# Float64 weights split in 480 columns instead of 576, with ScalarE and DMA copies taking part; gates multiplied by ScalarE

## The chip, the core and the metric

One core of a Trainium2 chip. The metric is the device time of one execution in microseconds; lower is better. TensorE (PE) multiplies matrices into PSUM, VectorE (DVE), ScalarE (ACT) and GpSimd (POOL) do elementwise work, SyncE (SP) issues DMAs. Every engine has a queue of its own and runs it in order; an instruction that waits holds up all that stand behind it.

## The reference

Three models run one after the other on 3072 tokens of 320 values: a recurrent attention, a mixture of eight experts with 1024 hidden units, and a gated feed-forward model with 1536 hidden units.

```python
def _moe_ref(x, modality_id, w_gate, modality_bias, w1, w2):
    logits = x @ w_gate + modality_bias[modality_id]
    e_idx = np.argmax(logits, axis=1)
    ...
    gate_w = probs[np.arange(N), e_idx]
    for e in range(E):
        mask = e_idx == e
        h = np.maximum(x[mask] @ w1[e], 0.0)
        out[mask] = gate_w[mask, None] * (h @ w2[e])
    return out

def _moe2_ref(x, w_gate, w_val, w_out):
    g = x @ w_gate
    silu = g * (1.0 / (1.0 + np.exp(-g)))
    val = x @ w_val
    return silu * val @ w_out
```

The weights of the last model (`w_gate`, `w_val`: 320 x 1536; `w_out`: 1536 x 320) come in as float64, because numpy's division by a square root makes them so.

## The kernel before

**Order.** The attention takes the first 560 us. Then the experts run in 32 passes `p` (eight slots of tokens, `sj`, by four quarters of the hidden units, `c`), until about 783 us, and then the gated model, in blocks of two or three tiles of 128 tokens and in passes `k` of 128 hidden units each. The program lists the instructions in an order written out by hand, and each engine takes its own from that list.

**Numbers in two parts.** Float32 values are multiplied on TensorE as a high part in a shorter format and the rest: three products of high and low each (`mm3`, lines 607 to 610). The 320 inputs are two blocks of 128 and one of 64; the last 64 fill only half of the partitions. There the high and the low part of `x` stand one above the other (`x2`), and the weights of these 64 inputs stand twice, once in each half of the partitions (`up`, lines 618 and 619). So the weights' third block has the same values in partitions 0 to 63 and 64 to 127.

**Splitting float64 weights.** `moe2_weights` (line 578) cuts each of `w_gate` (g) and `w_val` (v) into eight chunks of 192 hidden units, and `w_out` (o) into six. For each of these 22 chunks SyncE loads the raw words into a tile `st2` of which there are two (lines 591 to 596; the last 64 inputs are loaded twice, line 593), and `split64` (line 557) makes `hi` and `lo` in eight steps `o0` to `o7`. A float64 is two 32-bit words, `hw` and `lw`. ScalarE squares `hw` for a test against tiny values (line 566) and copies the result into the high part (line 572). VectorE builds the float32 from `hw` (567, 568, 571), makes a float of the top bits of `lw` by shifting and setting an exponent (569), takes the exponent (573), scales the low word by it (574), subtracts the high part (575) and adds both to the low part (576). The work tiles `cva`, `cvm`, `cvu` exist once. The load of chunk k+1 stands before step `o2` of chunk k. The steps are dealt out among the passes: in the experts' part by `prepare` (line 952), eleven chunks in all, and in the second model about four steps a pass, one between the cast `hh` (line 1120) and the difference `hl` (line 1124), the others behind it.

**Expert weights.** In each pass SyncE loads the weights of a later one (`load1`, `load2`), ScalarE casts them (line 668), and GpSimd or VectorE makes the difference (line 669). `evac` (line 928) takes the hidden units out of PSUM: ScalarE's Relu (930), VectorE's difference (931). PSUM has two tiles `pu` for hidden units, which the second model uses in turn for `pg` and `pv`: Silu (1115), product (1117), cast (1120), difference (1124).

**Gates.** A block's rows `xg` are gathered by GpSimd (line 973), the row's gate too (979), `gmul` (line 980) multiplies them on VectorE, and `xt2` has TensorE transpose the result (line 652). In the first block of the second model `gmul` and `xt2` for the next block stand in the passes 0 to 3.

Of the kernel before, what the change touches and what calls it, by code (L numbers as in the profile page):

```python
# [7 lines left out]
F32 = mybir.dt.float32  # L8
F32R = mybir.dt.float32r
BF16 = mybir.dt.bfloat16  # L10
I32 = mybir.dt.int32
AF = mybir.ActivationFunctionType
ALU = mybir.AluOpType
AX = mybir.AxisListType
# [487 lines left out]
def routing_constants(tc, keep, rc, mid, mbias):  # L502
# [3 lines left out]
    def tr(shape,name,dt=F32): C[name]=rc.tile(shape,dt,name="r"+name); return C[name]  # L506
    it=tr([128,128],"it",I32)
    G.iota(it[:],pattern=[[1,128]],base=0,channel_multiplier=0)
# [8 lines left out]
    h3=tk([128,NT],"h3",BF16); V.tensor_scalar(h3[:],it[:,0:NT],64.0,None,ALU.add)  # L517
    ip=tr([128,1],"ip",I32); G.iota(ip[:],pattern=[[0,1]],base=0,channel_multiplier=1)
    pp=tk([128,1],"pp"); V.tensor_copy(pp[:],ip[:])
# [8 lines left out]
    mi=tr([128,24],"mi",I32)  # L528
    nc.sync.dma_start(mi[:],mid.bitcast(I32).rearrange("(t p two) -> p t two",p=128,two=2)[:,:,0])
    bb=tr([128,2,8],"bb")  # L530
# [15 lines left out]
def choose(tc, C, LG, t0, t1):  # L546
# [7 lines left out]
    V.tensor_tensor(eq,eq,C['rev'][:].unsqueeze(1).to_broadcast([128,n,8]),ALU.mult)  # L554
    V.tensor_reduce(km,eq,AX.X,ALU.max)
    V.tensor_tensor(oh.rearrange("p e t -> p t e"),eq,bc(km),ALU.is_equal)
def split64(nc, P, raw, hi, lo, shape):

    V,A,G=nc.vector,nc.scalar,nc.gpsimd
    def t(n,dt=I32): return P.tile(shape,dt,tag="cv"+n,bufs=1,name="cv"+n)  # L560
    lw,hw=raw[:,:,:,0],raw[:,:,:,1]
    a,m,u=t("a"),t("m"),t("u")
    k=u[:].bitcast(F32)
    af,mf,uf=a[:].bitcast(F32),m[:].bitcast(F32),u[:].bitcast(F32)
    def o0():
        A.activation(k,hw.bitcast(F32),AF.Square)
        V.tensor_scalar(a[:],hw,3,0x3fffffff,ALU.logical_shift_left,ALU.bitwise_and)
    def o1(): V.scalar_tensor_tensor(a[:],hw,-0x40000000,a[:],ALU.bitwise_and,ALU.bitwise_or)
    def o2(): V.tensor_scalar(m[:],lw,9,0x3f800000,ALU.logical_shift_right,ALU.bitwise_or)
    def o3():  # L570
        V.scalar_tensor_tensor(af,k,3.4332275390625e-05**2,af,ALU.is_ge,ALU.mult)
        A.copy(hi,af)
    def o4(): V.tensor_scalar(u[:],a[:],-0x800000,None,ALU.bitwise_and)
    def o5(): V.scalar_tensor_tensor(mf,mf,-1.0,uf,ALU.add,ALU.mult)
    def o6(): (G if Q["G6"] else V).tensor_tensor(af,af,hi.bitcast(F32),ALU.subtract)
    def o7(): V.scalar_tensor_tensor(lo,mf,2.0**-20,af,ALU.mult,ALU.add)
    return [o0,o1,o2,o3,o4,o5,o6,o7]
def moe2_weights(tc, pool, stp, wg, wv, wo):

    nc=tc.nc  # L580
    W={}; T={}
    for nm,src in (("g",wg),("v",wv)):
        T[nm]=src.bitcast(I32).rearrange("k (f two) -> k f two",two=2)
        W[nm]=tuple(pool.tile([128,3,1536],F32R,name="w"+nm+x) for x in "hl")
    W["o"]=tuple(pool.tile([128,12,320],F32R,name="wo"+x) for x in "hl")
    T["o"]=wo.bitcast(I32).rearrange("k (f two) -> k f two",two=2)
    todo=[(nm,c) for c in range(8) for nm in "gvo" if nm!="o" or c<6]
    def step(k):
        nm,c=todo[k]; hi,lo=W[nm]; src=T[nm]
        if nm!="o":  # L590
            s=stp.tile([128,3,192,2],I32,tag="st2",name="st2"); cs=slice(192*c,192*c+192)
            nc.sync.dma_start(s[:,0:2],src[0:256,cs].rearrange("(k p) f two -> p k (f two)",p=128))
            for z in range(2): nc.sync.dma_start(s[64*z:64*z+64,2],src[256:320,cs])
            return lambda: split64(nc,stp,s,hi[:,:,cs],lo[:,:,cs],[128,3,192])
        s=stp.tile([128,2,320,2],I32,tag="st2",name="st2o"); cs=slice(2*c,2*c+2)
        nc.sync.dma_start(s[:],src[256*c:256*c+256].rearrange("(k p) f two -> p k (f two)",p=128))
        return lambda: split64(nc,stp,s,hi[:,cs],lo[:,cs],[128,2,320])
    def ops():
        nxt=step(0); yield
        for k in range(len(todo)):  # L600
            cur=nxt; nxt=None
            l=cur()
            for i,f in enumerate(l):
                if i==2 and k+1<len(todo): nxt=step(k+1)
                yield f
    return W,ops(),8*len(todo)
# [18 lines left out]
class Moe:  # L625
# [266 lines left out]
    def main(s, LG, y1, gd, wg, wv, wo, out):  # L892
        tc=s.tc; nc=s.nc; V,A,G,T=nc.vector,nc.scalar,nc.gpsimd,nc.tensor; C=s.C
        s.gd=gd
        with ExitStack() as ctx:
# [3 lines left out]
            P=ctx.enter_context(tc.tile_pool(name="m1",bufs=1)); s.wp.append(P)  # L899
# [7 lines left out]
            R={}; GX={}  # L907
# [43 lines left out]
            done=0  # L951
# [14 lines left out]
            XG={}; ID={}; GT={}; YP={}; YT=[]  # L966
# [13 lines left out]
            def gmul(b,i):  # L980
                if b>=len(blocks) or i>=len(blocks[b]): return
                h=blocks[b][i]; t=TILES[h]
                V.tensor_scalar(XG[b][i][:,0:320],XG[b][i][:,0:320],(GT[b][:,i:i+1] if h>=0 else R['gate'][:,t:t+1]),None,ALU.mult)
            def xt2(b,i):
                if b>=len(blocks) or i>=len(blocks[b]): return
                if i==0: X['b',b]=s.xspare(b) if 2<=b<HB else s.xalloc(NSTAT+b)
# [37 lines left out]
            for p in range(NP):  # L1024
                sj,c=divmod(p,4)
# [22 lines left out]
                if sj==NSTAT-1 and c<2: gmul(0,c)  # L1048
# [55 lines left out]
            k=0  # L1104
            for b,h in passes:
                n=128*len(blocks[b]); x=cut(X['b',b],n)
                for fc in ((0,1,2,3,4,5),(6,7,8,9,10,11),range(12))[h]:
# [3 lines left out]
                    while done<8*NEED[fc] and done<nbetween:  # L1111
                        f=next(between,None); done+=1
# [8 lines left out]
                    if done<need(2*NP+k):  # L1121
                        f=next(between,None); done+=1
# [87 lines left out]
```

## Time and profile before

| | |
|---|---|
| median of 3 runs | 1206.11 us (1204.70 to 1207.41) |
| the profiled execution | 1203.11 us |
| its span | 1201.4 us |
| busy: PE, DVE, ACT, POOL | 88%, 68%, 47%, 42% |

The span runs from the first to the last instruction recorded; the rest of an execution's time lies around it. In the rows below a name such as `hl<-pu,hh` says which tile an instruction writes and which it reads; `st` is a raw g or v chunk, `st2o` a raw o chunk, `woh` and `wol` the high and low part of `w_out`. A bracket gives the idle time before an instruction and the one that ended it. "issue" stands where no releaser was found. PEq, DVEq and SPq are sequencers.

### The profile page before, as it was taken

The page shows a single profiled execution, that of the slowest core. Times are in us where ns is not written, and L with a number is a line of the kernel's source. Part 1 is how long each engine was busy: PE and PEld are TensorE (multiplying, and loading weights), DVE is VectorE, ACT ScalarE, POOL GpSimd, SP SyncE. Part 2 cuts the span into 40 slices and gives each one's busy share as a digit, 9 for nine tenths or more (in the row PEclk, how much of TensorE's full clock was granted, in tenths as well). Part 3 has the DMA queues.
Part 4 walks back from the last instruction along what each step waited for, and adds up shares of the span by engine and source line. Part 5 has one row for each costly group of instructions (what it writes and reads, how often), then busy time and mean ns, then how long its engine had stood idle before and what let it go on. Part 6 is the DMA issues. An engine that isn't in the chain of part 4 may idle for free. (4 is left out here: it accounts for less than half of the span.)

```text
span 1201.4 us, 27833 instructions
## 1 busy us (share of the span) xinstructions
PE 1060.6 (88%) x10437; PEld 998.4 (83%) x10437; DVE 822.9 (68%) x2020; ACT 558.8 (47%) x1344; POOL 499.0 (42%) x1038
## 2 busy tenths in 40 slices
PE   5358799898988889897899899979999999999998
PEld 4247788887877778786789899979999999999998
DVE  5998888989889887753837987888952343333332
ACT  4346466756666674453435555444432222222332
POOL 7885666767666575512434343422000311201100
PEclk9668989998899999998999999999999999999999
DMA  5555346554644542330556577432100100100000
GB/s 97 85 91 95 71 79 118 102 118 82 136 98 95 104 89 66 77 86 22 172 150 179 176 212 223 135 107 86 60 1 11 40 22 23 34 1 28 17 24 12
DMA packets 278720, 102.88 MB, mean 86 GB/s; under 512 B 235728, under 2 KB 273360, under 8 KB 278576
## 3 DMA queue, kind: packets, MB, share of 16 engines
q1 hardware_dynamic: 271264, 86.05, 32.1%
q0 software_dynamic: 3856, 11.02, 3.1%
q10 hardware_dynamic: 3456, 3.93, 1.0%
q8 instruction: 86, 1.41, 0.5%
q14 instruction: 58, 0.48, 0.1%
HBM read 77.56 MB, written 23.40 MB: 84 GB/s over the span
## 5 line engine op out<-in xcount | busy, mean ns | idle before, releaser
L1117 DVE TENSOR_TENSOR s<-s,pu 128x384 f32<-128x384 f32 (+1 forms) x108 | 55.0, 509 | 157.3 <-PE pu L619 153.7
L266 POOL TENSOR_TENSOR tmp<-Lb,Pm 128x60 f32<-128x60 f32 (+22 forms) x348 | 107.5, 309 | 53.7 <-DMA Lb<-LD 27.7
L266 DVE TENSOR_TENSOR tmp<-Lb,Pm 128x60 f32<-128x60 f32 (+24 forms) x372 | 112.7, 303 | 19.2 <-DMA Lb<-LD 8.1
L1120 ACT CAST hh<-s 128x384 fp32r<-128x384 f32 (+1 forms) x108 | 51.6, 478 | 149.2 <-DVE s L1117 149.2
L1085 POOL DMA_INDIRECT out_dram<-ys,id x20 | 19.7, 987 | 234.2 <-DVE ys L1082 104.7
L269 DVE TENSOR_TENSOR Pm<-Pm,tmp 128x60 f32<-128x60 f32 (+24 forms) x372 | 108.6, 292 | 9.4
L669 POOL TENSOR_TENSOR l<-s,h 128x768 fp32r<-128x768 f32 (+1 forms) x32 | 59.4, 1859 | 133.8 <-ACT h L668 103.7
L269 POOL TENSOR_TENSOR Pm<-Pm,tmp 128x60 f32<-128x60 f32 (+22 forms) x348 | 102.8, 295 | 26.6 <-POOL tmp L266 0.3
L1115 ACT ACTIVATE s<-pu 128x384 f32<-128x384 f32 (+1 forms) x108 | 49.2, 456 | 112.4 <-PE pu L619 112.1
L608 PE MATMUL pd<-woh,hh 128*128 128x320 f32 x288 | 89.0, 309 | 0.1
L609 PE MATMUL pd<-woh,hl 128*128 128x320 f32 x288 | 89.1, 309 | 0.1
L610 PE MATMUL pd<-wol,hh 128*128 128x320 f32 x288 | 88.9, 309 | 0.0
L1124 DVE TENSOR_TENSOR hl<-s,hh 128x384 fp32r<-128x384 f32 (+1 forms) x108 | 55.4, 513 | 47.9 <-ACT hh L1120 47.4
L198 POOL TENSOR_TENSOR ks<-I,rawb 64x320 f32<-64x320 f32 x48 | 49.4, 1028 | 52.0 <-DVE I L194 30.0
L608 PE MATMUL pu<-xh,h 128*128 128x384 f32 (+1 forms) x128 | 48.8, 381 | 16.8 <-DVE hl L931 11.1
L668 ACT CAST h<-s 128x640 fp32r<-128x640 f32 (+1 forms) x64 | 49.6, 780 | 28.4 <-PE pd L609 9.6
L608 PE MATMUL pd<-h,hh 128*128 128x320 f32 x200 | 61.9, 310 | 0.0
L609 PE MATMUL pd<-h,hl 128*128 128x320 f32 x200 | 61.8, 309 | 0.0
L610 PE MATMUL pd<-l,hh 128*128 128x320 f32 x200 | 61.8, 309 | 0.0
L374 PE MATMUL pq<-rbd,VT 128*128 128x128 f32 x384 | 58.1, 300 | 0.0
L223 PE MATMUL sc<-kbt,atb 128*128 128x128 f32 x384 | 54.4, 296 | 3.6 <-ACT atb L209 2.8
L316 PE MATMUL zz<-pbd,MA 128*104 128x128 f32 x384 | 54.7, 290 | 2.5 <-ACT VU L138 1.0
(377 smaller groups left out, 3400.1 us busy)
## 6 DMA issues: line engine op xcount, KB each, us to landing
s<-in_moe_w_dram SPq DMA_DIRECT2D x32, 320.0 KB, 3.6
s<-in_moe_w_dram SPq DMA_DIRECT2D x32, 256.0 KB, 3.3
Lb<-LD SPq DMA_DIRECT2D x24, 256.0 KB, 3.7
y<-zrow SPq DMA_DIRECT2D x9, 483.0 KB, 4.7
s<-in_moe_w_dram SPq DMA_DIRECT2D x64, 64.0 KB, 3.3
raww<-in_w_dram SPq DMA_DIRECT2D x24, 160.0 KB, 3.3
rawa<-in_a_dram SPq DMA_DIRECT2D x24, 160.0 KB, 3.7
rawk<-in_k_dram SPq DMA_DIRECT2D x24, 160.0 KB, 2.8
```

The source lines that it names most:

```text
L223: T.matmul(ps[:,q].rearrange("p s j -> p (s j)"),ATB[0][:,4*c+q].rearrange("p s j -> p (s j)"),X[i,c][:,q],start=True,stop=True)
L266: E.tensor_tensor(tmp[:,0:k_,0:ni],Lb[:,j+1:32,j].unsqueeze(1).to_broadcast([128,k_,ni]), Pm[:,0:k_,j].unsqueeze(2).to_broadcast([128,k_,n ...
L269: E.tensor_tensor(Pm[:,0:k_,j+1:32],Pm[:,0:k_,j+1:32],tmp[:,0:k_,0:ni],ALU.add)
L316: T.matmul(ps[0:104,h],u['MA'][:,8*i+4*g+h,0:104],pbd[:,4*g+h],start=True,stop=True)
L374: T.matmul(pq[:,q],X['VT',c][:,q],RBD[0][:,q,cc].rearrange("p s t -> p (s t)"),start=True,stop=True)
L608: T.matmul(out,lh,rh,start=first,stop=False)
L609: T.matmul(out,ll,rh,start=False,stop=False)
L610: T.matmul(out,lh,rl,start=False,stop=last)
L669: (E or s.nc.gpsimd).tensor_tensor(hl[1][:],t[:],hl[0][:].bitcast(F32),ALU.subtract)
L1117: V.tensor_tensor(sg,sg,pv,ALU.mult)
L1120: A.copy(hh,sg)
L1124: V.tensor_tensor(hl,sg,hh.bitcast(F32),ALU.subtract)
```

## The change

The split of a g or v chunk works on 480 columns instead of 576: two blocks of 192, and the last 64 inputs as 96 columns, the first 96 hidden units in partitions 0 to 63 and the other 96 in partitions 64 to 127, so that nothing is split twice. The high part goes to a tile `sph` of its own (there is one), the low part of the first 384 columns straight into its place, and that of the 96 columns into the raw tile. SyncE then issues nine copies between SBUF tiles: one of the high part's 384 columns and four of its 96 columns (each half of the hidden units into each half of the partitions) after `o3`, and four of the low part's after `o7`. Step `o7` of a g or v chunk is two VectorE instructions, of 384 and of 96 columns. In all chunks, o too, ScalarE makes a float of the whole low word, read as an unsigned integer, in step `o0`, behind the Square; step `o2` is empty and the scale of `o5` is 2 to the power of -32. `gmul` is a ScalarE instruction.

```diff
--- before.py
+++ after.py
@@ -9,6 +9,7 @@
 F32R = mybir.dt.float32r
 BF16 = mybir.dt.bfloat16
 I32 = mybir.dt.int32
+U32 = mybir.dt.uint32
 AF = mybir.ActivationFunctionType
 ALU = mybir.AluOpType
 AX = mybir.AxisListType
@@ -554,26 +555,32 @@
     V.tensor_tensor(eq,eq,C['rev'][:].unsqueeze(1).to_broadcast([128,n,8]),ALU.mult)
     V.tensor_reduce(km,eq,AX.X,ALU.max)
     V.tensor_tensor(oh.rearrange("p e t -> p t e"),eq,bc(km),ALU.is_equal)
-def split64(nc, P, raw, hi, lo, shape):
+def split64(nc, P, raw, hi, lo, shape, done=None):
 
     V,A,G=nc.vector,nc.scalar,nc.gpsimd
     def t(n,dt=I32): return P.tile(shape,dt,tag="cv"+n,bufs=1,name="cv"+n)
-    lw,hw=raw[:,:,:,0],raw[:,:,:,1]
+    lw,hw=raw[...,0],raw[...,1]
     a,m,u=t("a"),t("m"),t("u")
     k=u[:].bitcast(F32)
     af,mf,uf=a[:].bitcast(F32),m[:].bitcast(F32),u[:].bitcast(F32)
     def o0():
-        A.activation(k,hw.bitcast(F32),AF.Square)
+        A.activation(k,hw.bitcast(F32),AF.Square); A.copy(mf,lw.bitcast(U32))
         V.tensor_scalar(a[:],hw,3,0x3fffffff,ALU.logical_shift_left,ALU.bitwise_and)
     def o1(): V.scalar_tensor_tensor(a[:],hw,-0x40000000,a[:],ALU.bitwise_and,ALU.bitwise_or)
-    def o2(): V.tensor_scalar(m[:],lw,9,0x3f800000,ALU.logical_shift_right,ALU.bitwise_or)
+    def o2(): pass
     def o3():
         V.scalar_tensor_tensor(af,k,3.4332275390625e-05**2,af,ALU.is_ge,ALU.mult)
         A.copy(hi,af)
+        if done: done[0]()
     def o4(): V.tensor_scalar(u[:],a[:],-0x800000,None,ALU.bitwise_and)
-    def o5(): V.scalar_tensor_tensor(mf,mf,-1.0,uf,ALU.add,ALU.mult)
+    def o5(): V.scalar_tensor_tensor(mf,mf,2.0**-32,uf,ALU.mult,ALU.mult)
     def o6(): (G if Q["G6"] else V).tensor_tensor(af,af,hi.bitcast(F32),ALU.subtract)
-    def o7(): V.scalar_tensor_tensor(lo,mf,2.0**-20,af,ALU.mult,ALU.add)
+    def o7():
+        for l,f in lo if done else ((lo,None),):
+            x,y=(mf,af) if f is None else (mf[:,f],af[:,f])
+            if f and f.start==0: x,y=(z.rearrange("p (k f) -> p k f",k=2) for z in (x,y))
+            V.scalar_tensor_tensor(l,x,2.0**-20,y,ALU.mult,ALU.add)
+        if done: done[1]()
     return [o0,o1,o2,o3,o4,o5,o6,o7]
 def moe2_weights(tc, pool, stp, wg, wv, wo):
 
@@ -588,10 +595,19 @@
     def step(k):
         nm,c=todo[k]; hi,lo=W[nm]; src=T[nm]
         if nm!="o":
-            s=stp.tile([128,3,192,2],I32,tag="st2",name="st2"); cs=slice(192*c,192*c+192)
-            nc.sync.dma_start(s[:,0:2],src[0:256,cs].rearrange("(k p) f two -> p k (f two)",p=128))
-            for z in range(2): nc.sync.dma_start(s[64*z:64*z+64,2],src[256:320,cs])
-            return lambda: split64(nc,stp,s,hi[:,:,cs],lo[:,:,cs],[128,3,192])
+
+            s=stp.tile([128,480,2],I32,tag="st2",name="st2"); cs=slice(192*c,192*c+192)
+            nc.sync.dma_start(s[:,0:384].rearrange("p (k f) two -> p k (f two)",k=2),src[0:256,cs].rearrange("(k p) f two -> p k (f two)",p=128))
+            for z in range(2): nc.sync.dma_start(s[64*z:64*z+64,384:480],src[256:320,192*c+96*z:192*c+96*z+96])
+            t=stp.tile([128,480],F32R,tag="sph",bufs=1,name="sph"); t2=s[:,384:432].rearrange("p f two -> p (f two)").bitcast(F32R)
+            def both(y,x):
+                for z in range(2):
+                    for q in range(2):
+                        nc.sync.dma_start(y[64*q:64*q+64,2,192*c+96*z:192*c+96*z+96].bitcast(F32),x[64*z:64*z+64].bitcast(F32))
+            def high():
+                nc.sync.dma_start(hi[:,0:2,cs].bitcast(F32),t[:,0:384].bitcast(F32).rearrange("p (k f) -> p k f",k=2))
+                both(hi,t[:,384:480])
+            return lambda: split64(nc,stp,s,t[:],((lo[:,0:2,cs],slice(0,384)),(t2,slice(384,480))),[128,480],(high,lambda: both(lo,t2)))
         s=stp.tile([128,2,320,2],I32,tag="st2",name="st2o"); cs=slice(2*c,2*c+2)
         nc.sync.dma_start(s[:],src[256*c:256*c+256].rearrange("(k p) f two -> p k (f two)",p=128))
         return lambda: split64(nc,stp,s,hi[:,cs],lo[:,cs],[128,2,320])
@@ -980,7 +996,7 @@
             def gmul(b,i):
                 if b>=len(blocks) or i>=len(blocks[b]): return
                 h=blocks[b][i]; t=TILES[h]
-                V.tensor_scalar(XG[b][i][:,0:320],XG[b][i][:,0:320],(GT[b][:,i:i+1] if h>=0 else R['gate'][:,t:t+1]),None,ALU.mult)
+                A.mul(XG[b][i][:,0:320],XG[b][i][:,0:320],(GT[b][:,i:i+1] if h>=0 else R['gate'][:,t:t+1]))
             def xt2(b,i):
                 if b>=len(blocks) or i>=len(blocks[b]): return
                 if i==0: X['b',b]=s.xspare(b) if 2<=b<HB else s.xalloc(NSTAT+b)
```

## Rows read from the trace of the kernel before

**Rows 1.** The page's forty slices of 30 us: busy tenths, and granted clock.

```profile
PE   5358799898988889897899899979999999999998
DVE  5998888989889887753837987888952343333332
PEclk9668989998899999998999999999999999999999
```

**Rows 2.** Stretch sums; columns: PE, PEld, DVE, ACT, POOL busy, PEclk, DMA share, GB/s.

```profile
740.00:750.00 10.00, 7.79 (x40) 7.52 (x40) 9.34 (x16) 3.53 (x7) 1.90 (x1) 0.83 0.84 249
783.00:810.00 27.00, 20.59 (x156) 19.16 (x154) 21.81 (x49) 11.38 (x26) 6.75 (x6) 1.00 0.39 108
890.00:1201.00 311.00, 307.47 (x2033) 306.64 (x2032) 107.66 (x236) 85.92 (x198) 40.85 (x42) 1.00 0.07 21
```

**Rows 3.** What TensorE waited for, 600 to 900 us: total, times, longest us.

```profile
PE pu L608 <- DVE hl L931: 8.2, 6, 2.3
PE xt L652 <- issue: 6.8, 5, 2.0
PE pu L608 <- ACT s L1115: 1.7, 2, 1.5
```

**Rows 4.** TensorE's timeline: start, length us; in brackets the idle before, releaser.

```profile
688.67 0.44 PE L608 MATMUL pu<-xh,h 128*128 128x384 f32 x1 [1.40 <-DVE hl L931]
745.50 0.44 PE L608 MATMUL pu<-xh,h 128*128 128x384 f32 x1 [2.21 <-DVE hl L931]
796.66 0.52 PE L652 MATMUL xt<-ident,xg 128*128 128x128 f32 x3 [1.75 <-issue]
```

**Rows 5.** VectorE by line: count, min/median/max ns, first and last start, forms.

```profile
L568 DVE SCALAR_TENSOR_TENSOR cva<-st,cva x16: 743/758/2347, 633.3 to 877.8; 128x576 int32<-128x576 int32 x16
L568 DVE SCALAR_TENSOR_TENSOR cva<-st2o,cva x6: 818/826/826, 658.4 to 843.0; 128x640 int32<-128x640 int32 x6
L569 DVE TENSOR_SCALAR cvm<-st x16: 445/453/515, 634.0 to 879.0; 128x576 int32<-128x576 int32 x16
L569 DVE TENSOR_SCALAR cvm<-st2o x6: 484/485/486, 662.7 to 844.4; 128x640 int32<-128x640 int32 x6
L983 DVE TENSOR_SCALAR xg<-xg,gt x20: 374/386/389, 765.4 to 1071.7; 128x320 f32<-128x320 f32 x20
```

**Rows 6.** ScalarE by line, the same columns.

```profile
L566 ACT ACTIVATE cvu<-st x16: 717/729/737, 632.0 to 874.6; 128x576 f32<-128x576 f32 x16
L566 ACT ACTIVATE cvu<-st2o x6: 774/782/799, 655.9 to 840.6; 128x640 f32<-128x640 f32 x6
L572 ACT CAST wgh<-cva x8: 672/674/678, 635.2 to 872.2; 128x576 fp32r<-128x576 f32 x8
L942 ACT COPY ys<-pd x16: 425/428/448, 605.0 to 787.7; 128x320 f32<-128x320 f32 x16
L819 ACT ACTIVATE H<-H,rpp x2: 759/760/760, 579.5 to 580.9; 128x552 bf16<-128x552 bf16 x2
```

**Rows 7.** Timelines of VectorE and GpSimd at 742 us.

```profile
741.95 2.28 DVE L576 SCALAR_TENSOR_TENSOR wvl<-cvm,cva 128x576 fp32r<-128x576 f32 x1
...
741.71 1.90 POOL L669 TENSOR_TENSOR l<-s,h 128x768 fp32r<-128x768 f32 x1 [2.31 <-ACT h L668]
```

**Rows 8.** Issue, line 593; then us to landing of lines 943 and 596.

```profile
L593 SPq DMA_DIRECT2D st<-in_moe_w_val_dram x16: 479/595/859, 623.6 to 863.5; - x16
...
DMA to landing us min/median/max: 2.1/2.9/3.6
...
DMA to landing us min/median/max: 4.0/5.1/7.6
```

**Rows 9.** VectorE's timeline: end of one chunk, start of the next but one.

```profile
804.46 0.76 DVE L576 SCALAR_TENSOR_TENSOR wgl<-cvm,cva 128x576 fp32r<-128x576 f32 x1
...
815.14 0.48 DVE L567 TENSOR_SCALAR cva<-st2o 128x640 int32<-128x640 int32 x1
```

**Rows 10.** DMA queue, 630 to 900 us: packets, MB, share of 16 engines.

```profile
q1 hardware_dynamic: 26128, 31.63, 39.1%
```

## Prediction

> **What bounds the kernel now.** I read the page's forty slices first [rows 1]: TensorE falls to seven tenths in slice 27 and is at nine from slice 28 on, and VectorE is at seven to nine tenths in slices 22 to 29, where the change's code runs. The stretch sums [rows 2] show that TensorE works 307.5 of the last 311 us, so nothing done there to the other engines can move the end; but in the first block of the second model, 783 to 810 us, it works 20.6 of 27 us while VectorE works 21.8. So I asked what TensorE waits for between 600 and 900 us [rows 3]: 8.2 us for `hl` of line 931, which frees the PSUM tile, 6.8 us before the transposes `xt`, put down to "issue" but standing behind the gate multiply that makes their input, and 1.7 us for the Silu. That is 16.7 us, all that a lighter VectorE can give. Single waits [rows 4] show where: 1.40, 2.21, 1.75 us. Everything after 823 us moves with the sum of what is saved before.
>
> **What VectorE loses.** Its eight split instructions have two rates [rows 5]: two-tensor ones (lines 568, 571, 574, 575, 576) take 758 ns at 576 columns and 826 at 640, 1.06 ns a column, so 656 at 480, 554 at 384, 248 at 96; the scalar ones (567, 569, 573) take 453 and 485, so 405 at 480. A g or v chunk costs 5 x 758 + 3 x 453 = 5149 ns. Afterwards: 4 x 656, 554 + 248 for line 576 cut in two, 2 x 405, line 569 gone: 4236 ns. That is 0.913 us less on each of 16 chunks, 14.6 us; the six o chunks lose line 569's 485 ns, 2.9 us; eleven of the 24 gate multiplies at 386 ns lie before 890 us, 4.2 us. VectorE gets 21.7 us lighter while it matters. Most of that lies beside TensorE's work and saves nothing; only what stands in front of a wait counts.
>
> **What ScalarE gains.** The Square falls from 729 to 649 ns (0.83 ns a column from its two rows [rows 6]), the cast to `hi` from 674 to 594. The conversion of the low word isn't in the trace; its nearest row is the Square, which reads the same strided words: 649 ns at 480, 782 at 640. If conversion from unsigned integers cost nothing extra it could be as short as the cast, 594; the other bound is twice the Square, 1.3 us. I take 649. Per g or v chunk ScalarE gets 0.49 us more, per o chunk 0.78. The gate multiply lies between the plain copy of 320 columns, 428 ns, and line 819's multiply by a per-partition scale, 760 ns at 552 columns, so 567 at 320; I take 567, the same form. ScalarE works 11.4 of 27 us in the first block [rows 2], so the time is there; its order is what can cost.
>
> **The sum, 632 to 783 us.** I followed VectorE's queue back from each `hl` wait to the last point where it idled, and subtracted the split instructions between: 0.5 us at 675, 0.25 at 681, 0.85 at 689 (a whole g chunk stands there, and the wait is 1.40), 0.53 at 695, 0.24 at 703, 0.2 at 745, 0.4 at 766: 3.0 us. At 766 the transposes would no longer wait 1.6 us for the multiply, but `hl` of line 931 frees the PSUM tile 0.4 us later and is late next.
>
> At 745 VectorE's line 576 took 2.28 us because GpSimd's line 669 began just before it [rows 7]; other VectorE instructions of two SBUF tensors stretch likewise. The Trainium skill (SBUF — State Buffer, Who interferes with whom) says that the two engines lock a shared port pair for a whole instruction and that the first to issue wins; the trace agrees in this pair. By that rule cutting line 576 in two opens a gap in which GpSimd may get in, an estimated 1.9 us when it does; by my sum, without it, the cut costs 0.04 us a chunk.
>
> **The sum, 783 to 823 us.** The wait of 0.81 us at 791 grows by 0.4: the multiply now stands on ScalarE behind the cast to `hi`, itself behind VectorE's line 571 (0.73 + 0.57 against the 0.39 and 0.49 saved). At 797 the multiply no longer stands behind three split instructions on VectorE; the 1.75 us go but for 0.25, where `s` of line 1117 is late next: 1.5. At 802, line 569 and the shorter forms save 0.7 and the move another 0.7: 1.4. The Silu waits at 806 to 810 have 1.28 us of removed work in front of them: 1.2. Together 1.5 + 1.4 + 1.2 - 0.4 = 3.7 us. The wait of 0.67 us at 823 is for the gathered gate itself and stays, now on ScalarE with the next Silu queued behind it.
>
> **What the new order takes back.** Nine more DMAs a chunk go through SyncE: five wait for `hi`, four for the low part; queued behind them are the expert weights, the y stores and the next split loads. An issue took 0.48 to 0.86 us, 0.595 in the median [rows 8], so 2.9 and 2.4 us a chunk. Behind the five, an expert load can start some 5 us late; in the timelines it is issued 8 to 10 us before its cast and lands within 5 to 6.5. I count zero there and 2 us for the range. The narrow low part now lies in the raw tile, of which there are two, so the load of chunk k+2 starts only when the four copies of chunk k have landed. No row shows such a copy; the nearest is the y store from SBUF, 2.9 us (2.1 to 3.6) [rows 8]. The chain is 4 x 0.595 + 2.9 + 0.4 + 5.1 us for an o chunk: 10.8, with ends of 1.9 + 2.1 + 0.4 + 4.0 = 8.4 and 2.4 + 3.6 + 0.4 + 7.6 = 14.0. From the end of line 576 at 805.22 to line 567 two chunks on at 815.14 there are 9.9 us [rows 9]. So a load comes between 1.5 us early and 4 us late, likely 0.9 late, for seven chunks in the second model. There the Square and line 567 wait with Silu and `s` behind them; TensorE has some 2 us of slack a pass after 810 us (its timeline puts 2.7 us of other matmuls before it needs a PSUM tile back), none before. I take 1.5 us. Last, the conversion must wait for line 576 of the chunk before (the same tile), with Relu or Silu behind it; mostly VectorE is the late one anyway. Bounds 0 and 22 x 0.65 = 14 us; I take 0.7, about one conversion on the path, since in most cases the `hl` that follows is behind the same VectorE queue.
>
> Net: 3.0 + 3.7 - 1.5 - 0.7 = 4.5 us. The profiled execution ran 1203.1 us, its span 1201.4 and 1.7 around it; the median lies 3.0 above. Span 1196.9, execution 1198.6, median 1206.1 - 4.5 = 1201.6 us.
>
> **Rivals.**
> - All of VectorE's waits go. For it: 21.7 us are taken off VectorE against 16.7 us of waits, and the 2.21 us wait at 745 is followed by some 4 us of matmuls at the lower clock level, 1.2 GHz (granted clock 0.83 in 740 to 750 [rows 2]), which might go with it. Against: the other waits have less than their length of split work in front. Gain 11 to 15 us: 1191 to 1195.
> - ScalarE takes VectorE's place. Conversion and multiply stand in front of Relu and Silu and wait for VectorE; seven conversions on the path at 0.65 us eat the 4.5. Time 1204 to 1208, no change. Against: ScalarE is busy 11.4 of 27 us where it would matter [rows 2].
> - Slower: the chain of copies and loads sets the pace. The place is the Square of each chunk in the second model; it decides from a chain longer than 9.9 us plus 2 us of slack. At 14.0 us seven chunks lose 2 us each, 14 us, less 3 of the gain left: 1217; at 13 us, 1210. For it: an o load took up to 7.6 us. Against: it needs long copies and long loads together, and the queue carries less after 783 us. All packets of the SP queue between 630 and 900 us, 1.2 KB in the mean, took 39.1% of the engines' time [rows 10], 65 ns each; the new ones are shorter. The Trainium skill (DMA: Bandwidth & Descriptors, Specifications) puts full rate at 512 bytes and above and says that shorter ones read and write back; eight of the nine copies move runs of 384 bytes. No row shows such copies between SBUF tiles; by that rule this rival gets likelier.
> - It doesn't do what it says: a conversion at 1.3 us makes ScalarE's extra 22 x 0.65 = 14 us; this goes with the second rival.
>
> **How the numbers follow.** Forecast (gain 2.4 to 11 us) 0.46, all waits gone 0.09, no change 0.19, the chain slower 0.20, expert loads late behind SyncE's copies so that split casts stall 0.06 (1209 to 1215). Faster by over 0.2% (2.4 us, about what a measurement of this kernel can tell from no change) 0.55, same 0.19, slower 0.26. The range from 1193 to 1212 leaves out half of the full gain (0.05) and half of the slow cases (0.13). The forecast's own range is 1195 to 1203.7.
>
> **What would show it.** Right: line 569 and 983 gone from VectorE, its two-tensor instructions near 656 ns, TensorE's `hl` and `xt` waits between 632 and 823 us down from 15 to about 8 us, no waits added after 823. Wrong: the Square waiting for `st` DMAs by microseconds each chunk; conversions above 0.7 us; Relu, Silu or casts behind them with TensorE waiting for ScalarE; expert-weight casts waiting for DMAs.

## Result and the profile after

The changed kernel takes 1211.55 us in the median of five runs (1211.24 to 1213.91), the kernel before beside it 1204.70 us (1202.35 to 1207.41): the ratio is 1.0058, 95% interval 1.0039 to 1.0077. It is slower by 5 to 9 us where 4.5 us of gain were forecast. The time lies inside the range given, but the sign is wrong. The profiled execution ran 1211.24 us with a span of 1209.5, against 1201.4 before.

The lines of this kernel are shifted: Relu and `hl` of 930 and 931 are 946 and 947, the cast and the difference of an expert's weights (668, 669) are 684 and 685, their loads (661, 662, 665) are 677, 678 and 681. The nine copies are line 608 (the 384 columns of the high part) and line 606 (the four of the high part's and the four of the low part's 96 columns).

The stretch sums of after for the experts' last part and the turn to the second model; columns as in [rows 2]:

```profile
630.00:783.00 153.00, 137.44 (x822) 134.40 (x821) 114.54 (x209) 81.55 (x167) 57.52 (x37) 0.96 0.64 187
783.00:830.00 47.00, 42.17 (x276) 40.48 (x276) 35.20 (x79) 23.68 (x53) 12.45 (x13) 0.96 0.44 123
830.00:1000.00 170.00, 170.00 (x1073) 169.92 (x1072) 87.27 (x182) 62.16 (x135) 22.82 (x24) 1.00 0.17 49
```

The first two before:

```profile
630.00:783.00 153.00, 143.12 (x883) 139.90 (x883) 128.70 (x227) 80.23 (x163) 61.41 (x40) 0.99 0.61 181
783.00:830.00 47.00, 39.92 (x272) 38.24 (x271) 39.44 (x85) 20.19 (x45) 14.02 (x12) 1.00 0.37 107
```

Both executions reach the first cast of an expert's weights at the same time, 540.8 us before and 540.4 after, so these stretches hold about the same part of the program. VectorE got lighter by 18.4 us as meant, and yet TensorE did 61 matmuls fewer in the experts' part and only 4 more in the next. From 600 to 830 us it is 48 fewer (the 30 us from 600 on have 146 and 155); at 0.162 us each (143.12 / 883) that is 7.8 us, about all of the 8.1 us between the spans (a few records of matmuls can be missing). After 830 us TensorE works without a gap in both. In the experts' part 5.7 us of the loss is more idle time (15.6 instead of 9.9), and some 4 us are the slower clock: a matmul took 0.167 us instead of 0.162 in the mean. In stretches of 10 us the granted clock, a mean of its two levels of 1.2 and 2.4 GHz, is 0.83 from 690 to 710 us, where TensorE works 7.2 of the first 10 us, and 0.75 from 760 to 770 us, where it works 6.5; before, only 740 to 750 us lies below 1.00 between 630 and 783 us [rows 2].

What TensorE waited for from 630 to 830 us, what ScalarE waited for from 630 to 900 us, and what SyncE's queue waited for from 630 to 783 us, where expert loads stand in it (total, times, longest us; some lines of each):

```profile
PE pu L624 <- DVE hl L947: 10.4, 9, 2.8
PE pu L624 <- DVE id L994: 3.5, 1, 3.5
PE xt L668 <- ACT xg L999: 2.7, 2, 1.9
```

```profile
ACT h L684 <- DMA s<-in_moe_w_dram: 20.5, 13, 3.3
ACT cvm L567 <- DVE st L582: 8.5, 7, 2.6
ACT cvu L567 <- DMA st<-in_moe_w_gate_dram: 4.5, 3, 2.9
```

```profile
SPq L608 <- ACT hh L946: 11.5, 2, 8.9
SPq L608 <- ACT x L638: 10.1, 4, 4.8
SPq L606 <- DVE hl L947: 3.4, 2, 1.8
```

Two lines of ScalarE's waits before, from 630 to 900 us:

```profile
ACT h L668 <- DMA s<-in_moe_w_dram: 0.3, 1, 0.3
ACT wgh L572 <- DVE cva L571: 18.1, 8, 5.4
```

The first line of the second fence is the new thing: the cast `h` of an expert's weights waits 20.5 us for its load, where before it waited 0.3 us, once. The third says why the load is late: the copies stand at the head of SyncE's queue, waiting for the cast that makes what they copy (the releasers named are what ScalarE did around it), up to 8.9 us at a time and 32.9 us in all. That cast, to the high part, was late before too, as it waited for VectorE up to 5.4 us; but then no DMA stood in SyncE's queue to wait with it. The `hl` waits did not fall (8.2 us in [rows 3]), and the wait of 3.5 us, TensorE's longest, is one more of them: the copy `id` of line 994 that the row names is what VectorE did just ahead of `hl`. The `xt` waits fell from 6.8 to 2.7 us.

One case from end to end, from the timelines of GpSimd, VectorE, ScalarE, SyncE and TensorE:

```profile
675.92 1.84 POOL L685 TENSOR_TENSOR l<-s,h 128x768 fp32r<-128x768 f32 x1 [5.60 <-ACT h L684]
676.51 1.93 DVE L685 TENSOR_TENSOR l<-s,h 128x640 fp32r<-128x640 f32 x1 [0.34 <-ACT h L684]
679.58 0.70 DVE L572 SCALAR_TENSOR_TENSOR cva<-cvu,cva 128x480 f32<-128x480 f32 x1
680.31 0.59 ACT L573 CAST sph<-cva 128x480 fp32r<-128x480 f32 x1 [3.84 <-DVE cva L572]
680.93 0.66 SPq L608 DMA_DIRECT2D wgh<-sph  x1
681.64 2.54 SPq L606 DMA_DIRECT2D wgh<-sph  x4
684.43 0.38 SPq L677 DMA_DIRECT2D s<-in_moe_w_dram  x1
689.67 0.83 ACT L684 CAST h<-s 128x768 fp32r<-128x768 f32 x1 [3.26 <-DMA s<-in_moe_w_dram]
691.82 1.31 DVE L685 TENSOR_TENSOR l<-s,h 128x640 fp32r<-128x640 f32 x1 [2.62 <-ACT h L684]
697.39 0.69 PE L624 MATMUL pu<-xh,h 128*128 128x384 f32 x1 [2.83 <-DVE hl L947]
```

VectorE's difference `l` takes 1.93 us instead of 0.82 (e13 below) because GpSimd's began 0.59 us earlier; so line 572 is late by about 1.1 us, ScalarE's cast to the high part waits 3.84 us for it, the copies wait for the cast and then take 3.25 us to issue (680.93 to 684.18), and only then does the expert load start. Its cast waits 3.26 us, VectorE's next `l` then 2.62 us for the cast behind that one, and TensorE 2.83 us for the `hl` that VectorE makes after it. From 630 to 783 us VectorE's waits for these casts are 30.6 us, against 16.6 before. The chain that ended last, by engine, shows the same in one line:

```profile
PE 38%; DVE 4%; DMA 2%; ACT 2%; SPq 2%; issue 1%; POOL 0%; ACTq 0%; DVEq 0%; POOLq 0%
```

Before it was 43% TensorE, 1% DMA and 0% SyncE.

### The profile page after: what moved, and what is told of

Its sections match the earlier page's. It is cut to its first block, busy times and chain, and to the rows that moved or that the text cites. A ratio compares the mean times of both kernels' runs of the same rounds, so it can differ in the third digit from the quotient of the medians.

```text
span 1209.5 us, 28147 instructions
## 1 busy us (share of the span) xinstructions
PE 1061.2 (88%) x10437; PEld 999.9 (83%) x10437; DVE 800.7 (66%) x1990; ACT 578.7 (48%) x1390; POOL 498.5 (41%) x1038
## 5 line engine op out<-in xcount | busy, mean ns | idle before, releaser
L685 POOL TENSOR_TENSOR l<-s,h 128x768 fp32r<-128x768 f32 (+1 forms) x32 | 58.7, 1836 | 143.6 <-ACT h L684 120.6
L684 ACT CAST h<-s 128x640 fp32r<-128x640 f32 (+1 forms) x64 | 49.1, 781 | 36.0 <-DMA s<-in_moe_w_dram 22.6
L685 DVE TENSOR_TENSOR l<-s,h 128x640 fp32r<-128x640 f32 (+1 forms) x32 | 40.1, 1255 | 37.2 <-ACT h L684 37.1
```

The lines of the kernel that those rows point to most:

```text
L684: s.nc.scalar.copy(hl[0][:],t[:])
L685: (E or s.nc.gpsimd).tensor_tensor(hl[1][:],t[:],hl[0][:].bitcast(F32),ALU.subtract)
```

## Experiments

Two questions: what lost the time (runs e1 to e8), and why a lighter VectorE did not win any (e9 to e15). For the first, theory A is that the nine copies do it, by A1, their waits at the head of SyncE's queue with the expert loads behind them; A2, the time that their issue takes; or A3, their traffic. Theory B is that ScalarE, with the conversion and the gates, takes VectorE's place. All were timed beside the kernel before (1204.2 to 1205.9 us); a ratio is to that.

### Each part alone

`e1_low`: the low word on ScalarE, whole chunks of 576 columns.

```diff
-        A.activation(k,hw.bitcast(F32),AF.Square)
+        A.activation(k,hw.bitcast(F32),AF.Square); A.copy(mf,lw.bitcast(U32))
-    def o2(): V.tensor_scalar(m[:],lw,9,0x3f800000,ALU.logical_shift_right,ALU.bitwise_or)
+    def o2(): pass
-    def o5(): V.scalar_tensor_tensor(mf,mf,-1.0,uf,ALU.add,ALU.mult)
+    def o5(): V.scalar_tensor_tensor(mf,mf,2.0**-32,uf,ALU.mult,ALU.mult)
```

> Of the three parts of the change this kernel has one: ScalarE makes the float of the low word, at 576 columns, in place; no copies, gates on VectorE. If SyncE's copies make the loss (theory A), this part gains what step o2 took on VectorE in front of TensorE's waits: 1200 to 1204 us against 1204.7. If the loss is ScalarE's conversion waiting for the step o7 before, with Relu and Silu behind it (theory B; in the changed kernel such waits sum to 12 us), it is 3 to 8 us slower than before: 1208 to 1213.

`e2_gate`: the gate multiply alone is moved (`V.tensor_scalar` becomes `A.mul` in `gmul`).

> Only the gate multiply goes to ScalarE. Before, TensorE's transposes waited 6.8 us behind it, in the changed kernel 2.7 us. Theory A and my prediction: 2 to 4 us faster, 1201 to 1203 us. Theory B (ScalarE is the late engine): no change or slower, 1205 to 1208 us.

`e3_lowgate`: both, without the narrow split and its copies.

> Low word and gates on ScalarE, 576 columns, no copies: the whole of ScalarE's new work without SyncE's. Theory A: faster than before by 3 to 6 us, 1199 to 1202 us, so that the copies cost about 10 us of the changed kernel's 1211.6. Theory B: 1208 to 1213 us, near the changed kernel.

`e4_cols480`: the split of 480 columns with its nine copies alone; low word and gates stay on VectorE, as before.

> Only the split in 480 columns with its nine copies a chunk; low word and gates on VectorE as before. Theory A (copies, by their place in SyncE's queue or by their traffic): slower than before by 5 to 12 us, 1210 to 1217 us, with the casts of expert weights waiting some 20 us for their loads as in the changed kernel. Theory B: no slower than before, 1200 to 1205 us, since VectorE has 0.43 us less work a chunk.

Measured: e1 1206.31 us, 1.0000 (0.9984 to 1.0015); e2 1204.63, 0.9995 (0.9978 to 1.0012); e3 1205.61, 1.0001 (0.9982 to 1.0020); e4 1213.18, 1.0066 (1.0040 to 1.0092). The split in 480 columns with its copies carries the whole loss; what ScalarE took over costs nothing that can be measured. It brings nothing that can be measured either, so the gains that theory A counted on in e1 to e3 (1199 to 1204 us) did not come. Theory B falls. In e4 the casts' wait for expert loads is as in the changed kernel:

```profile
ACT h L684 <- DMA s<-in_moe_w_dram: 25.7, 17, 3.4
```

### What in the copies

`e5_defer`: the changed kernel, but the copies are put in a list, which is issued behind the next pass's expert loads, or at the latest ahead of the next split load and, in the second model, at the start of a pass.

```diff
-            return lambda: split64(nc,stp,s,t[:],((lo[:,0:2,cs],slice(0,384)),(t2,slice(384,480))),[128,480],(high,lambda: both(lo,t2)))
+            return lambda: split64(nc,stp,s,t[:],((lo[:,0:2,cs],slice(0,384)),(t2,slice(384,480))),[128,480],(lambda: late.append(high),lambda: late.append(lambda: both(lo,t2))))
...
-                load1(p+3); load2(p+2)
+                load1(p+3); load2(p+2); W["flush"]()
```

> The changed kernel, but each group of copies is issued later: behind the next pass's expert loads (in the second model, at the next pass's start), when its data are long there, and at the latest before the next split load. SyncE then hardly waits for ScalarE or VectorE at a copy; issue time and bytes are the same. If the loss comes from copies that wait at the head of SyncE's queue with expert loads behind them (A1), most of it goes: 1204 to 1207 us. If it is the 5.4 us of issue a chunk (A2) or the bytes on the DMA engines (A3): 1209 to 1213 us, as the changed kernel's 1211.6.

`e6_dummy`: e3 with nine needless copies a chunk of about the same sizes (354 columns for the 384), from a constant into a tile that nobody reads, in the same places of SyncE's queue. They wait for no engine.

```diff
-            return lambda: split64(nc,stp,s,hi[:,:,cs],lo[:,:,cs],[128,3,192])
+            return lambda: split64(nc,stp,s,hi[:,:,cs],lo[:,:,cs],[128,3,192],(high,both))
+                nc.sync.dma_start(dst[64*q:64*q+64,354+96*z:354+96*z+96],one[64*z:64*z+64,0:96])
```

> The kernel with low word and gates on ScalarE and 576 columns (1205.6 us), with nine needless copies a g or v chunk at the same places, of about the same shapes, from a constant tile to a tile that nobody reads: they never wait. It adds issue time and traffic alone. A1: 1204 to 1208 us. A2 or A3: 1209 to 1213 us.

`e7_dummy_small`: the same copies with one column each.

> As the kernel with needless copies, but each moves one column instead of 96 or 354: the same nine issues, hardly any bytes. A2 (issue time): the same as with the wide needless copies, within 1 us. A3 (bytes): back to 1205 to 1206 us while the wide ones stay above 1209. A1: both near 1206.

`e8_actq`: the changed kernel with its nine copies issued by ScalarE (`nc.scalar.dma_start` for `nc.sync.dma_start`), the low part's behind the next conversion.

> The changed kernel with all nine copies issued from ScalarE's queue instead of SyncE's: the high part's right behind the cast that makes it, the low part's behind the next chunk's conversion, which waits for the same step anyway. SyncE's queue is as before the change. A1 and A2: the casts of expert weights wait for DMAs for less than 3 us in sum (20.5 us in the changed kernel), and the time is 1203 to 1208 us unless ScalarE's own issues delay Relu and Silu, in which case TensorE's waits name ScalarE. A3: casts still wait and 1210 us or more.

Measured: e5 1203.99 us, 0.9988 (0.9971 to 1.0004); e6 1206.24, 1.0000 (0.9985 to 1.0014); e7 1206.61, 1.0007 (0.9993 to 1.0020); e8 1273.77, 1.0568 (1.0539 to 1.0597). The needless copies all write one tile, so some wait for an earlier copy: 7.6 us in six waits of 1.8 us at most, from 630 to 830 us. Still they cost nothing that can be measured, so neither their issue in SyncE's queue nor their traffic is the loss (A2 and A3 fall); nor do the real ones once the expert loads stand in front of them. What costs is that they wait there, ahead of those loads: A1. The casts' wait in e5:

```profile
ACT h L689 <- DMA s<-in_moe_w_dram: 4.3, 3, 1.9
```

e8 takes the copies out of SyncE's way and pays more on ScalarE. Its timeline, with the sequencer's issues:

```profile
652.35 0.59 ACT L574 CAST sph<-cva 128x480 fp32r<-128x480 f32 x1 [1.46 <-DVE l L689]
652.98 0.66 ACTq L612 DMA_DIRECT2D wvh<-sph  x1
653.68 2.84 ACTq L610 DMA_DIRECT2D wvh<-sph  x4
656.55 0.37 ACT L642 CAST xh<-xt 128x256 fp32r<-128x256 f32 x1 [3.61 <-DMA wvh<-sph]
```

Five issues hold ScalarE for 3.61 us with the casts that TensorE needs behind them; its `hl` waits are 31.2 us. The casts of expert weights wait only 0.4 us for their loads there, so the expert loads are in time; the same issues that cost nothing in SyncE's queue (e6) are dear on an engine that TensorE waits for. They are not all of e8's loss: SyncE's loads of o chunks wait 62.7 us for copies from the raw tile, and no run separates the two.

### Why a lighter VectorE won nothing

In e3 VectorE has the relief and nobody loses; still TensorE's `hl` waits between 630 and 830 us are 10.2 us, against 8.2 before.

Fixed times don't hold the same part of the program in every run. The first cast of an expert's weights, up to which the listed instructions are the same in all, starts at 540.8 us before and at 546.7 in e3 (539.8 to 546.7 over all runs); nothing here shows why. From that cast to the end of the span the one profiled execution of each kernel took 660.6 us before, 669.1 changed, 658.7 in e3, 647.0 in e9, 650.3 in e13 and 648.1 in e14. So e3's relief may be worth 2 us, which its interval can't tell from nothing.

VectorE's groups of 632 to 783 us (count, busy us, mean ns, idle before), of e3 and of the kernel before:

```profile
L670 DVE TENSOR_TENSOR l<-s,h 128x640 fp32r<-128x640 f32 x24 | 29.6, 1235 | 17.0 <-ACT h L669 16.7
```

```profile
L669 DVE TENSOR_TENSOR l<-s,h 128x640 fp32r<-128x640 f32 x24 | 25.6, 1065 | 16.7 <-ACT h L668 16.6
```

The difference `l`, which takes 820 ns where GpSimd makes none (e13), took 1065 in the mean before, 1088 in e2, 1203 in e1, 1235 in e3 and 1419 in the changed kernel: with less to do ahead of it, VectorE comes to it sooner and falls more often under GpSimd's `l`, which starts when ScalarE's cast ends. Of the 5.1 us that line 569 had cost there (8 x 459 and 3 x 485 ns), 4.0 us went into longer `l`. But other instructions were stretched less for it. Count for each shape of VectorE's two-tensor instructions from 630 to 783 us its number times its mean, less the smallest mean of that shape in any run: in sum they are stretched by 14.1 us before, 14.3 in e1, 15.1 in e3 and 13.5 in the changed kernel. So the collision moved to `l`, which stands in front of `hl`, and hardly grew.

Theory "order" says that this collision takes back what VectorE is relieved of; theory "size" says that the relief was only too small. `e9_lighter_v` is e3 with three more instructions left out (lines 569, 574 and 575: `o1`, `o4` and `o5` become `pass`).

> From e3_lowgate (low word and gates on ScalarE, whole chunks split, no copies) with three more of VectorE's split instructions left out: the one of line 569 that joins the sign bit to the shifted word, and lines 574 and 575, which scale the low word; the weights' values are therefore wrong. ScalarE, GpSimd and the order of all that is left stay. Off VectorE: 0.754 + 0.455 + 0.752 = 1.96 us per g or v chunk and 0.83 + 0.49 + 0.83 = 2.15 per o chunk, some 18 to 20 us in 632 to 783 us and 44 us in all. Theory 'order' (VectorE's saved time in 632 to 783 us does not reach TensorE: VectorE comes earlier to the difference l of the second expert matrix, and there waits for ScalarE's cast or falls under GpSimd's 1.86 us difference that has just begun, so hl starts hardly earlier): VectorE's idle time in 630 to 783 us up from 28 to over 40 us, its l difference (1235 ns mean in e3) no shorter, hl waits of line 932 between 630 and 783 us still above 5 us (10 in e3), ratio to before 0.996 to 1.000. Theory 'size' (what my sum counted: each hl wait shrinks by the split work taken away in front of it, the first 5 us were only too few): hl waits under 2 us, TensorE's work in 630 to 783 us up from 143 to 149 us or more, 1196 to 1199 us, ratio 0.990 to 0.994.

`e10_pieces_before` and `e11_pieces_defer` issue GpSimd's difference in three pieces:

```diff
-        (E or s.nc.gpsimd).tensor_tensor(hl[1][:],t[:],hl[0][:].bitcast(F32),ALU.subtract)
+        if E: E.tensor_tensor(hl[1][:],t[:],hl[0][:].bitcast(F32),ALU.subtract)
+        else:
+            for k in range(t.shape[1]): s.nc.gpsimd.tensor_tensor(hl[1][:,k],t[:,k],hl[0][:,k].bitcast(F32),ALU.subtract)
```

> The kernel before with one edit: GpSimd's difference l of an expert's first matrix (128x768, 1.86 us) is issued as three of 128x256, some 0.65 to 0.75 us each. Theory 'order': VectorE's two-tensor instructions of two SBUF tiles that start beside GpSimd's wait at most for one third of it, then run between the pieces; the 14 to 15 us by which VectorE's instructions are stretched in 630 to 783 us fall to 5 to 9, l's mean falls from 1065 to under 950 ns, hl waits from 8.2 to 4 to 6 us, 1201 to 1204 us, ratio 0.996 to 0.999. Rival 'no matter which engine is first' (every piece stretches the VectorE instruction beside it, the pieces' fixed cost makes GpSimd longer): stretched time unchanged, ratio 0.999 to 1.002.

> e5_defer (the change with its nine copies issued behind the expert loads) with GpSimd's difference l in three pieces, as in e10_pieces_before. Theory 'order': what VectorE was relieved of now reaches TensorE, since the collision that took it back is shorter: l's mean from 1320 to under 1000 ns, hl waits of 9.5 us between 600 and 830 us to under 5, 1197 to 1201 us, ratio 0.993 to 0.997, and more gained than by the pieces alone. Rival: as e5_defer, 1203 to 1205 us.

`e12` to `e15` give GpSimd's difference to VectorE, in four kernels (`V1` lists the passes in which VectorE makes it):

```diff
-'V1': (3,)
+'V1': range(32)
```

> e5_defer with the first matrix's difference l on VectorE instead of GpSimd, in all passes: no collision with GpSimd is left there, VectorE gets 24 instructions of 128x768, some 0.97 us each by the 1.06 ns a column of its two-tensor instructions, 23 us more in 630 to 783 us, less the 15 us of stretching: 8 us heavier net. Theory 'order' (collisions, not VectorE's total, are what hl waits for): no l above 1.1 us, hl waits not above 9.5 us, 1201 to 1205 us. Theory 'size': 8 us more work on VectorE makes hl waits rise to 12 to 16 us, 1206 to 1211 us.

> The kernel before with one edit: the first matrix's difference l on VectorE in all passes, GpSimd does none of them. VectorE gets 24 x 0.95 = 22.8 us in 632 to 783 us and loses 14.5 us of stretching, 8 us more net. Theory 'order' (the collision hid what a lighter VectorE is worth): the collision goes here too but VectorE has the whole split and the gates still to do, so 1198 to 1202 us, ratio 0.995 to 0.998, hl waits of 5 to 7 us, and e14 is faster by at least 3 us. Theory 'move alone' (the change's relief of VectorE is worth nothing even now): as e12, 1194 to 1197 us, ratio 0.991 to 0.994.

> e3_lowgate (low word and gates on ScalarE, whole chunks split, no copies) with the first matrix's difference l on VectorE in all passes. Theory 'order': faster than e13 by 3 to 6 us, ratio 0.990 to 0.994, hl waits of 3 to 5 us. Theory 'move alone': within 1.5 us of e13.

> The changed kernel as it is, its nine copies waiting in SyncE's queue ahead of the expert loads, with the first matrix's difference l on VectorE in all passes. If the copies' waits cost as much by themselves: 5 to 9 us over e12, 1201 to 1205 us, the casts' wait for expert loads 15 us or more between 630 and 900 us. If the loss came only together with the collision: 1195 to 1198 us.

Measured, with TensorE's `hl` waits from 630 to 830 us:

| kernel | median us | ratio (95%) | `hl` waits us |
|---|---|---|---|
| e9: e3, VectorE lighter still | 1191.98 | 0.9889 (0.9865 to 0.9912) | 4.8 |
| e10: before, pieces | 1199.95 | 0.9969 (0.9949 to 0.9989) | 5.1 |
| e11: e5, pieces | 1202.57 | 0.9986 (0.9970 to 1.0001) | 10.0 |
| e12: e5, all on VectorE | 1195.33 | 0.9927 (0.9903 to 0.9951) | 3.1 |
| e13: before, all on VectorE | 1194.33 | 0.9922 (0.9901 to 0.9943) | 2.2 |
| e14: e3, all on VectorE | 1191.70 | 0.9896 (0.9874 to 0.9918) | 1.9 |
| e15: changed, all on VectorE | 1206.24 | 1.0015 (0.9997 to 1.0032) | 13.2 |

e9 went against "order" in its time: a relief of some 20 us does reach TensorE, though `l` stays at 1257 ns and VectorE idles 47 of the 153 us from 630 us on, as "order" had it. Of e3's smaller relief nothing shows; whether it is lost in the noise or taken back by the collision, no run decides. e10's ratio, `hl` waits and mean `l` (941 ns) came out as "order" had them. e12 was faster than either theory had it (1201 to 1205 and 1206 to 1211 us), and e13, at 1194 us, as "move alone" had it, by which the change's relief is worth nothing even without the collision. e13's first stretch:

```profile
630.00:783.00 153.00, 149.68 (x951) 146.73 (x950) 139.31 (x268) 85.84 (x175) 19.95 (x20) 1.00 0.63 188
```

VectorE is 10.6 us heavier than before in the first stretch (139.31 against 128.70) and TensorE still does 68 matmuls more. VectorE's two-tensor instructions were stretched by 14.1 us in all before, and by 0.4 us here, and its waits for casts fell from 16.6 to 4.4 us: the new work fills time that VectorE had lost. The move does two things, since the first matrix's difference itself also falls from 1881 to 953 ns. That GpSimd was merely slow is not the reason, or not all of it: no wait of TensorE before names GpSimd's `l`, and in e10 GpSimd's difference takes 58.7 us in that stretch instead of 41.4, and the kernel is still faster, with VectorE's two-tensor instructions stretched by 9.0 us. e11 should have shown the same on e5 and did not; its `l` on VectorE is short, 986 ns, but other instructions are stretched for it (13.6 us in all, against 15.1 in e5), waits for ScalarE's cast rose to 22.6 us and one `hl` wait was 3.8 us. Why is left open.

Whether the change's relief is worth something with the collision gone is not shown: e14 is 2.6 us below e13, timed beside it, but their intervals overlap; I had set 3 us for "order" and 1.5 for "move alone", and it fell between. And the copies cost more than ever: e15 is 14.5 us above e14, TensorE doing 139.6 us of work in 630 to 783 us instead of 150.8, with the casts waiting 24.7 us; 15 us or more were set for that wait, and 1201 to 1205 us for the time, which came out at 1206.24. e12, whose copies stand behind the loads, is 3.6 us above e14, which has none, but not timed beside it and with intervals that overlap: what the moved copies still cost is not shown. e14 beats both kernels; its first stretch:

```profile
630.00:783.00 153.00, 150.84 (x957) 148.37 (x955) 134.95 (x251) 93.12 (x186) 20.52 (x19) 1.00 0.61 185
```

## Why the prediction was wrong

**What bounds the kernel** held: the difference arose before 830 us; from there to 1000 us TensorE works 170.0 of 170 us in the changed kernel as before.

**The prices** held. VectorE by line from 600 to 900 us, and ScalarE by line (min/median/max ns):

```profile
L572 DVE SCALAR_TENSOR_TENSOR cva<-cvu,cva 128x480 f32<-128x480 f32 x16 | 10.5, 656 | 0.4
```

```profile
L567 ACT CAST cvm<-st x16: 605/628/652, 631.2 to 884.9; 128x480 f32<-128x480 uint32 x16
L567 ACT CAST cvm<-st2o x6: 766/782/805, 659.7 to 850.0; 128x640 f32<-128x640 uint32 x6
L999 ACT ACTIVATE xg<-xg,gt x20: 557/565/569, 768.5 to 1078.8; 128x320 f32<-128x320 f32 x20
```

656 ns were predicted for a two-tensor step, 649 and 782 for the conversion, 567 for the multiply. They were measured at 656, 628 and 782, and 565. VectorE got 21.1 us lighter from 630 to 1000 us (128.70 + 39.44 + 90.01 against 114.54 + 35.20 + 87.27), where 21.7 were set for 632 to 890 us. The rival with dear conversions falls.

**The step that failed** is the one of the copies in SyncE's queue: "Behind the five, an expert load can start some 5 us late ... I count zero there and 2 us for the range". I had the place right, and the 8 to 10 us between a load's issue and its cast, but priced only the time of the issue. That part is small: five issues take 3.2 us, and in e6 nine of them, which hardly wait, cost nothing that can be measured. What I left out is the wait ahead of the issue: a copy holds the queue until the cast or `o7` that it copies from is done, 8.9 us at the longest, and that cast in turn waits for VectorE. My cover of 8 to 10 us, less 5 to 6.5 for landing, left some 3 us; it was gone 13 times. Even by my own figures a start 5 us late was more than those 3 us, so the zero had no reason behind it. The rival "expert loads late behind SyncE's copies so that split casts stall" was this one, with 1209 to 1215 us and a chance of 0.06; the time came out at 1211.55. That it also lies inside the range from 1193 to 1212 us is owed to the slow rivals, half of which the range took in, and not to the sum. The profile of before already had the pattern that should have raised it: SyncE's queue there waited too, 47.0 us at line 592 for VectorE's line 569, all of it after 783 us, where no expert load is left in the queue. And the last sign of being wrong that I named, expert-weight casts waiting for DMAs, is the one that came.

**632 to 783 us, 3.0 us of gain:** not seen. I followed each `hl` wait back and subtracted the split work ahead of it, which takes for granted that the rest stays as long as it was. It does not: `l` grew as VectorE came earlier (4.0 us in e3), though the stretching in all grew by only 1.0 us, so this accounts for a part at most. Here the Trainium skill (SBUF — State Buffer, Who interferes with whom), cited in the prediction for line 576, speaks of just this case: whoever of the two starts first holds the port pair for the whole instruction. The trace agrees: GpSimd's `l` at 675.92 ends at 677.76, and VectorE's, begun beside it, ends 0.68 us later. One row before does not fit: line 567, with one input from SBUF, took 2.25 us at 760.83 us instead of 0.46, beside a difference of GpSimd's that is recorded as starting 0.07 us later. I applied the rule to the cut of `o7` and not to the instruction that meets GpSimd in each pass. The cut itself was harmless: none of the 16 short parts was stretched in the changed kernel (255 ns at most), one of them in e5 (1893 ns).

**783 to 823 us, 3.7 us of gain:** partly seen. The `xt` waits fell by 4.1 us, and TensorE did 2.3 us more work in 783 to 830 us; but with the granted clock at 0.96 these are only 4 matmuls more, less than 1 us. In e2, e1 and e3 nothing of it can be measured at the end.

**What was taken back, 1.5 and 0.7 us:** the waits exist (7.6 us for split loads in five waits, 12.0 us of conversions for `o7` in nine, over the whole kernel), and no run separates what they cost TensorE; e1, with the conversion alone, says that it is little. The rival of the chain of copies and split loads is not what happened: after 830 us TensorE has no gap, and the loss lies in the experts' part.

## To carry to other kernels

A DMA that waits for an engine's result holds up everything behind it in its queue, so price such a transfer by its wait at the head of the queue, and put it behind the prefetches of the next pass; its issue and its bytes cost nothing that could be measured here. Before counting what a relieved engine gives back, look at which of its instructions are stretched by another engine: giving GpSimd's difference to VectorE, which ended the collision, gained 9.8 us (e13) with more work on VectorE, while the change's relief alone (e3) gained nothing that could be measured, and some 20 us more taken off (e9) gained 12.7 us with the collision still there. A load's slack before its use has to be compared with the sum of all waits in front of it, not with one.

## What the hardware showed that was not expected

- ScalarE's conversion from unsigned 32-bit words to float, every other word, costs no more than a Square of the same size and little more than a cast: 628 ns at 480 columns beside 646 for the Square and 593 for the cast to the high part.
- 92 copies of 384-byte runs between SBUF tiles and 11 of 472-byte runs, from 630 to 830 us, made no difference to copies of 4 bytes a run (e6 and e7: 1206.24 and 1206.61 us), and neither is clear of e3, which has no copies (1205.61 us). The Trainium skill (DMA: Bandwidth & Descriptors, Specifications) makes runs under 512 bytes the slow ones. All of these runs are shorter, so the pair does not test the limit; beside e3 it shows that such copies, when nothing waits for them, don't reach the time in a way that can be measured.
- A DMA issue takes ScalarE's queue for 0.61 us as it does SyncE's for 0.60; with the 144 of them on ScalarE the kernel took 70 us longer than with them behind the expert loads (e8 1273.77, e5 1203.99 us), their waits and those behind them included.
